# One key load, one copy of the small weights and a new instruction order in a fused sigmoid-attention and token-mixing kernel

## The chip, the cores and the metric

The kernel runs on one core of one Trainium2 chip. The metric is device time in microseconds (us). The profile names the engines PE (TensorE matmul), PEld (TensorE weight load), ACT (ScalarE), DVE (VectorE), POOL (GpSimd) and SP (SyncE, which issues most of the DMAs).

## What is computed

There are 8 batches and 12 heads, 448 tokens and a head size of 64. With `x` the heads side by side (8 x 448 x 768):

```
attn  = sigmoid(q k^T / 8 - log 448)            per batch and head
x     = attn v
W_tok = (x w_q)(x w_k)^T / 8                    w_q, w_k: 768 x 64
out   = relu(W_tok^T x) w_out                   w_out: 768 x 768
```

Inputs and outputs are fp32; the matmuls take bf16.

## The kernel before

The work comes in 24 **pairs**: two batches by two heads, 4 batch pairs with 6 head pairs each. A pair's q, k and v are one 448 KB DMA each (128 partitions, two runs of 1792 bytes per partition). POOL casts each to bf16 (line 118). q and k are then turned on PE (7 transposes of 128x128, line 131) and copied out of PSUM by DVE (line 138).

**Score blocks, S.** A pair has 7. Each is four 64x64 matmuls (one for each half of the rows and columns of the array, line 154) into a PSUM tile of 128x896; ACT makes the sigmoid of it in one instruction (line 159). The text numbers them S0 to S167. **Value blocks, P**, also 7 a pair and also four 64x64 matmuls (line 173), accumulate `attn v`.

After six pairs a batch pair goes through the mixing stage: `x` turned (x, 8 transposes, line 191), the projections W (four 64x64 matmuls each, 12 a batch pair, line 215), N (8 transposes, line 227), U (8 matmuls of 128x64, line 240), M (four 64x64 matmuls, line 264; `m` is the same with the relu on ACT), and O, the product with `w_out` (six 128x128 matmuls of 384 columns, line 283), 14 a batch pair.

**The order on every engine is the order in which the code is written.** A string, `PLAN`, has one letter for each step in PE's order: S, P, q and k (transposes), K (the second part of the first keys' transposes), x, W, N, U, M, O. It has 25 lines, and lines 0 to 23 each hold the 7 S of one pair; line 24 is what remains after the last S. The text speaks of these lines by number.

**PSUM** has three two-bank tiles, shared by S, P, W and M, and two one-bank tiles for the rest.

**Loads.** A second list, `ORDER`, is the order in which SP issues loads and POOL casts them. There are three fp32 buffers for each of q, k and v, so the load of key n waits until key n-3 is cast; there are two bf16 buffers for q and k, so the cast of key n waits until key n-2 has been transposed. SP and POOL take the list strictly in order: a load or cast that must wait holds all that stand behind it. `p_qk` (line 61) holds the transposed q and k.

`w_q` and `w_k` are loaded twice, once into each half of the partitions, with the two halves swapped in columns (lines 326 to 332), and cast at line 406. In the first pair the keys come in two DMAs (lines 352 and 353), of 3 and 4 of the 7 column groups, and are cast in the same two parts by POOL (line 421).

Of the kernel before, what the change touches and what calls it, by code (L numbers as in the profile page):

```python
# [9 lines left out]
F32 = mybir.dt.float32  # L10
# [6 lines left out]
def kernel(  # L17
# [18 lines left out]
    nc = tc.nc  # L36
    B, H, S, HD = q.shape
# [3 lines left out]
    P = 128  # L41
    NI, NP = 7, 64
# [4 lines left out]
    HALF = (slice(0, 64), slice(64, 128))  # L47
# [5 lines left out]
    def pool(name, bufs, **kw):  # L53
        return ctx.enter_context(tc.tile_pool(name=name, bufs=bufs, **kw))

    singles = pool("singles", 1)
# [1 line left out]
    p_w32 = pool("w32", 2)  # L58
    p_c16 = pool("c16", 2)
    p_v16 = pool("v16", 3)  # L60
    p_qk = pool("qk", 8)
    p_at = pool("at", 16)
    p_x = pool("x", 1)
    p_one = pool("one", 1)
# [10 lines left out]
    def bank2(name):  # L75
        n = free2.pop(0)
        return n, ps_q.tile([P, 2, 512], F32, tag=n, name=name)
# [4 lines left out]

    wout16 = singles.tile([P, NC, D], BF16, name="wout16")
    wqk16 = singles.tile([P, H, P], BF16, name="wqk16")
    wqk32 = singles.tile([P, H, P], F32, name="wqk32")
    ident = singles.tile([P, P], F32)
    bias_t = singles.tile([P, 1], F32)
    warm = singles.tile([P, 1], F32)
# [9 lines left out]
    N = len(pairs)  # L98
# [16 lines left out]
    def cast1(n, nm, eng):  # L115
        p = p_v16 if nm == "v" else p_c16
        t16 = p.tile([P, NI, 2, HD], BF16, tag=nm + "16", name=nm + "16")
        eng.tensor_copy(  # L118
            out=t16.rearrange("p i b d -> p b i d"),
            in_=ld.pop((nm, n)).rearrange("p b (i d) -> p b i d", i=NI),  # L120
        )
        ld[nm + "16", n] = t16


    qk = {}
# [24 lines left out]
    def scores(n, i):  # L150
        fb, sc = bank2("sc")
        for b2 in range(2):
            for h in range(2):
                nc.tensor.matmul(  # L154
                    sc[HALF[h], b2, 0:S], qk["k", n][HALF[b2], h, i, :],
                    qk["q", n][HALF[b2], h].rearrange("p i n -> p (i n)"), start=True, stop=True,
                )
        at = p_at.tile([P, 2, S], BF16, tag="at", name="at")
        nc.scalar.activation(at, sc[:, :, 0:S], ACTF.Sigmoid, bias=bias_t, scale=attn_scale)  # L159
        free2.append(fb)  # L160
        ats[n, i] = at
# [46 lines left out]
    def mlp_wqk(u, h):  # L208

        if h == 0:  # L210
            pw[u] = bank2("pw")
        fb, ps = pw[u]
        for b2 in range(2):
            for x in range(2):
                nc.tensor.matmul(  # L215
                    ps[HALF[x], b2, 0:S], wqk16[HALF[b2], h, 64 * x : 64 * x + 64],
                    xts[h // 2][HALF[b2], h % 2, 0:S], start=(h == 0), stop=(h == H - 1),
                )
        if h == H - 1:
            nc.vector.tensor_copy(out=wqk[:, :, 0:S], in_=ps[:, :, 0:S])  # L220
            free2.append(fb)

    def mlp_wkn(u):
        fb, ps = bank([P, 4, 2, P], BF16, "pk")
        for b2 in range(2):
            for m in range(4):
                nc.tensor.transpose(ps[:, m, b2, :], wqk[:, b2, m * P : (m + 1) * P], ident16)  # L227
        wkn[u] = p_one.tile([P, 4, P], BF16, tag="wkn", name="wkn")
        nc.vector.tensor_copy(
            out=wkn[u], in_=ps.rearrange("p m b x -> p m (b x)")[:, :, 64:192]  # L230
        )
        free1.append(fb)
# [91 lines left out]
    w32 = {}  # L324

    def load_weights():
        for b2 in range(2):
            for x, w in enumerate((moe_w_q, moe_w_k)):
                o = 64 * (x ^ b2)
                nc.sync.dma_start(  # L330
                    out=wqk32[HALF[b2], :, o : o + 64], in_=w.rearrange("(h d) n -> d h n", d=HD)
                )

    def load_wout(c):
        w32[c] = p_w32.tile([P, D], F32, tag="w32", name="w32")
        nc.sync.dma_start(out=w32[c], in_=moe_w_out[c * P : (c + 1) * P, :])

    IA, IB = slice(0, 4), slice(4, 7)  # L340
    KA, KB = slice(0, 3), slice(3, 7)
    q0 = p_ld.tile([P, 2, NI * HD], F32, tag="q32", name="q32")
    k0 = p_ld.tile([P, 2, NI * HD], F32, tag="k32", name="k32")
    src = {
        nm: SRC[nm][0:2, 0:2].rearrange("b h (p i) d -> (h p) b (i d)", i=NI) for nm in "qk"
    }

    def cols(r):
        return slice(r.start * HD, r.stop * HD)

    nc.sync.dma_start(out=q0, in_=src["q"])
    nc.sync.dma_start(out=k0[:, :, cols(KA)], in_=src["k"][:, :, cols(KA)])
    nc.sync.dma_start(out=k0[:, :, cols(KB)], in_=src["k"][:, :, cols(KB)])
    nc.vector.memset(zeros, 0.0)
    nc.vector.memset(bias_t, attn_bias)
    nc.gpsimd.memset(ident, 0.0)
# [1 line left out]
        out=ident, in_=ident, compare_op=ALU.not_equal, fill=1.0, base=0,  # L358
# [4 lines left out]
    fb, ps = bank2("pwarm")  # L363
# [4 lines left out]
        nc.vector.memset(t[:, :, S:], 0.0)  # L368


    ORDER = [("q", 1), ("k", 1), ("v", 0)]
    nq = 2
    for n in range(1, N):
        for _ in range(2 if n in (1, 2, 3, 4) else 1):
            if nq < N:
                ORDER += [("q", nq), ("k", nq)]
                nq += 1
        ORDER.append(("v", n))
    for n, at_ in ((0, 18), (1, 30), (2, 33), (3, 36), (4, 39), (5, 42), (6, 45)):
        ORDER.insert(at_, ("w", n))  # L380
    used, loaded, cast = set(), set(), set()

    def pump_loads():
        while len(loaded) < len(ORDER):
            nm, n = ORDER[len(loaded)]
            if nm == "w":
                if n >= 3 and ("w", n - 2) not in cast:
                    break
                load_wout(n - 1) if n else load_weights()
            else:  # L390
                if n >= 3 and (nm, n - 3) not in cast:
                    break
                load1(n, nm, nc.sync)
            loaded.add((nm, n))

    def pump():

        while len(cast) < len(ORDER) + 2:
            nm, n = ORDER[len(cast) - 2]
            if (nm, n) not in loaded:  # L400
                break
            if nm == "w":
                if n:
                    nc.gpsimd.tensor_copy(out=wout16[:, n - 1, :], in_=w32[n - 1])
                else:
                    nc.gpsimd.tensor_copy(out=wqk16, in_=wqk32)
            else:
                back = 3 if nm == "v" else 2
                if n >= back and (nm, n - back) not in used:
                    break  # L410
                cast1(n, nm, nc.gpsimd)
            cast.add((nm, n))
            pump_loads()
# [6 lines left out]
    for t16, t32, r, e in ((q016, q0, IA, "v"), (q016, q0, IB, "s"), (k016, k0, KA, "g"), (k016, k0, KB, "g")):  # L420
        COPY[e](
            out=t16[:, r].rearrange("p i b d -> p b i d"),
            in_=t32[:, :, cols(r)].rearrange("p b (i d) -> p b i d", d=HD),
# [4 lines left out]
    def tr_part(nm, t16, r, e, b=None):  # L428
# [15 lines left out]
    pump()  # L444

    PLAN = (  # L450
        "SSSKqSSSSkq",
        "SPPPPPSkSSPkSPqSS",
        "SxPqSPPPPSPPSqSPPSkPSPP",
        "SxPSSPkSSSkPPSkP",
        "SPPPPSqSqSSqxSxSk",
        "SSqkPPSPPPPSPqSkSSxPPPP",
        "SPPPSkqSWWWSWWWWSWWWWSWSx",
        "SNPSPPPPSPPSUSqSMUmSMq",
        "SkSMxSkSPPPSPPPPSqSk",
        "SMxmqSPPPPSPPPSOSSSOO",  # L460
        "SSkxSSOkSPPPSPPPPSO",
        "SSSqOkSPPPSPPPPSqxSPPPP",
        "SPPPSOSSSqOxSWWWWWSWW",
        "SWWWWWSOSSSNxPPPPPSPPSUU",
        "SMSxkSPPPPSPPPSOSMSkO",
        "SMmOkSMSOqSMSqOSPPPPSPPP",
        "SOSSSkOxSPPPSPPPPSxO",
        "SSSOOSSxOSPPSPPPPPPPPP",
        "SPPPSxqSWSWWWWWWSWWWSWWOS",
        "SSONSSOxSPPPPPPSPSUU",  # L470
        "SSMxOSSPPPPPPPSOSMSkx",
        "SPPPSPPPPmOSMmqOSMSOqSS",
        "SkOxSPPPPSPPPSOSSSOOx",
        "SPSPPPPPPSOSSSOOxS",
        "WPPPWPPPPWWWWWWWWWWOONxOUUMmmOOmMmOOOOOOOOOOOOOOOO",
    )
    done = dict.fromkeys("SPqkKxWNUMO", 0)
    done["q"] = done["k"] = 1

    for t in "".join(PLAN).replace(" ", ""):  # L480
        kind = "M" if t == "m" else t
        c = done[kind]
        done[kind] += 1
        tail = done["S"] == N * NI
        if t == "S":
            scores(*divmod(c, NI))
        elif t == "P":
            n, i = divmod(c, NI)
            values(n, i)
            if i == NI - 1:  # L490
                used.add(("v", n))
                pump()
        elif t in "qk":
            tr(c, t)
            used.add((t, c))
            pump()
        elif t == "K":
            tr_part("k", k016, KB, "v")
        elif t == "x":
            tr_x(c)  # L500
        elif t == "W":
            mlp_wqk(*divmod(c, H))
        elif t == "N":
            mlp_wkn(c)
        elif t == "U":
            mlp_tmp(*divmod(c, 2), tail and c % 2)
        elif kind == "M":
            u, x = divmod(c, NC)
            mlp_mix(u, x, t == "m")
            if x == NC - 1:  # L510
                chunks.extend((u, m, nb) for m in range(NI) for nb in range(2))
        elif t == "O":
            out_chunk(tail)
# [29 lines left out]
```

## Time and profile before

| | |
|---|---|
| median of 7 runs | 210.3 us (209.49 to 212.01) |
| the profiled execution | 210.7 us, span of its instructions 208.9 us |
| PE busy | 197.5 us, 95% of the span |
| ACT busy | 170.6 us, 82%, of it sigmoids 155.2 us (168 of them) |
| DVE, POOL busy | 121.8 us, 72.5 us |
| mean granted TensorE clock | 0.984 |
| q, k, v loads | 24 of each, 448 KB, 7.5 to 8.0 us from issue to landing (median) |

The span begins with the first instruction and ends when the last output has landed. Of the page, the slices (40 of 5.2 us) show how an engine fills over time, the groups give the duration of one instruction, and the chain of waits shows what followed what.

### The profile page before, as it was taken

The page shows a single profiled execution, that of the slowest core. Times are in us where ns is not written, and L with a number is a line of the kernel's source. Part 1 is how long each engine was busy: PE and PEld are TensorE (multiplying, and loading weights), DVE is VectorE, ACT ScalarE, POOL GpSimd, SP SyncE. Part 2 cuts the span into 40 slices and gives each one's busy share as a digit, 9 for nine tenths or more (in the row PEclk, how much of TensorE's full clock was granted, in tenths as well). Part 3 has the DMA queues.
Part 4 walks back from the last instruction along what each step waited for, and adds up shares of the span by engine and source line. Part 5 has one row for each costly group of instructions (what it writes and reads, how often), then busy time and mean ns, then how long its engine had stood idle before and what let it go on. Part 6 is the DMA issues. An engine that isn't in the chain of part 4 may idle for free.

```text
span 208.9 us, 6320 instructions
## 1 busy us (share of the span) xinstructions
PE 197.5 (95%) x2630; PEld 117.9 (56%) x2630; DVE 121.8 (58%) x208; ACT 170.6 (82%) x193; POOL 72.5 (35%) x85
## 2 busy tenths in 40 slices
PE   7489998999999999999999999999999999999991
PEld 7244544666556555656656565656565555655561
DVE  2234645774698755664889674645788654554321
ACT  4687999999999999999998989889888998055220
POOL 2477636877787833730022700251110000000000
PEclk9957999999999999999999999999999999999999
DMA  6999999999999999996064563355213362154785
GB/s 195 374 387 378 380 156 307 384 381 385 383 385 385 380 381 384 397 389 241 5 210 111 158 179 75 78 155 186 58 22 78 75 154 72 23 138 101 201 202 176
DMA packets 28684, 47.59 MB, mean 228 GB/s; under 512 B 5360, under 2 KB 24432, under 8 KB 28656
## 3 DMA queue, kind: packets, MB, share of 16 engines
q1 hardware_dynamic: 27616, 45.03, 67.1%
q10 hardware_dynamic: 1040, 2.16, 2.8%
q8 instruction: 20, 0.33, 0.7%
q14 instruction: 8, 0.07, 0.1%
HBM read 36.18 MB, written 11.01 MB: 226 GB/s over the span
## 4 chain that ended last, share of the span: by engine, by line
PE 83%; ACT 7%; DMA 3%; issue 2%; POOL 2%; SPq 1%; DVE 1%; DVEq 0%; ACTq 0%; POOLq 0%
PE po L283 27%; PE sc L154 18%; PE pv L173 14%; ACT at L159 7%; PE px L191 5%; PE ptq L131 5%; PE ptk L131 4%; PE pw L215 3%; DMA q<-in_q_dram 3%; PE pt L240 3%; PE pm L264 2%; POOL q L118 1%; PE pk L227 1%; DVE o L308 1%; POOL v L118 0%
## 5 line engine op out<-in xcount | busy, mean ns | idle before, releaser
L159 ACT ACTIVATE at<-sc,bias_t 128x896 bf16<-128x896 f32 x168 | 155.2, 1027 | 12.5 <-PE sc L154 11.6
L283 PE MATMUL po<-wout,mx 128*128 128x384 bf16 (+1 forms) x342 | 60.6, 324 | 0.0
L154 PE MATMUL sc<-qt,kt 64*64 64x448 bf16 x672 | 57.6, 364 | 2.8 <-ACT at L159 1.9
L283 PEld LDWEIGHTS <-mx 128*128 128x128 bf16 x342 | 30.9, 98 | 24.3 <-issue 7.0
L173 PE MATMUL pv<-at,v 64*64 64x448 bf16 x672 | 42.7, 358 | 0.3 <-POOL v L118 0.2
L178 DVE CAST xt<-pv 128x896 bf16<-128x896 f32 x24 | 26.2, 1091 | 23.0 <-PE pv L173 23.0
L308 DVE COPY o<-po 128x384 f32<-128x384 f32 x45 | 25.1, 557 | 24.7 <-PE po L283 24.4
L154 PEld LDWEIGHTS <-kt 64*64 64x64 bf16 x672 | 22.3, 105 | 24.2 <-issue 13.3
L118 POOL CAST q<-q 128x896 bf16<-128x896 f32 x23 | 21.5, 933 | 34.2 <-issue 26.3
L118 POOL CAST v<-v 128x896 bf16<-128x896 f32 x24 | 22.3, 934 | 22.5 <-PE pv L173 18.0
L118 POOL CAST k<-k 128x896 bf16<-128x896 f32 x23 | 21.5, 933 | 21.3 <-PE ptk L131 17.7
L173 PEld LDWEIGHTS <-v 64*64 64x64 bf16 x672 | 20.9, 108 | 10.3 <-issue 1.2
L138 DVE COPY kt<-ptk 128x896 bf16<-128x896 bf16 x23 | 14.2, 619 | 10.3 <-PE ptk L131 10.2
L196 DVE COPY xn<-px 128x512 bf16<-128x512 bf16 x48 | 18.0, 416 | 3.1 <-PE px L191 3.0
L306 ACT COPY o<-po 128x384 f32<-128x384 f32 x10 | 4.8, 478 | 15.7 <-PE po L283 15.7
L138 DVE COPY qt<-ptq 128x896 bf16<-128x896 bf16 x23 | 14.1, 618 | 5.7 <-PE ptq L131 5.3
L256 DVE TENSOR_SCALAR mx<-pm 128x896 bf16<-128x896 f32 x15 | 16.3, 1088 | 1.8 <-PE pm L264 1.4
L131 PE MATMUL ptq<-ident,q 128*128 128x128 bf16 x161 | 13.3, 224 | 2.7 <-POOL q L118 2.7
L191 PE MATMUL px<-ident,xt 128*128 128x128 bf16 x192 | 14.7, 220 | 0.2 <-DVE o L308 0.2
L191 PEld LDWEIGHTS <-xt 128*128 128x128 bf16 x192 | 11.6, 98 | 4.7 <-issue 3.9
L131 PEld LDWEIGHTS <-q 128*128 128x128 bf16 x161 | 9.6, 99 | 8.0 <-issue 3.7
L131 PE MATMUL ptk<-ident,k 128*128 128x128 bf16 x161 | 13.7, 228 | 0.0
(43 smaller groups left out, 93.7 us busy)
## 6 DMA issues: line engine op xcount, KB each, us to landing
q<-in_q_dram SPq DMA_DIRECT2D x24, 448.0 KB, 7.7
v<-in_v_dram SPq DMA_DIRECT2D x24, 448.0 KB, 7.5
k<-in_k_dram SPq DMA_DIRECT2D x23, 448.0 KB, 8.0
out_dram<-o SPq DMA_DIRECT2D x44, 192.0 KB, 3.0
w<-in_moe_w_out_dram SPq DMA_DIRECT2D x6, 384.0 KB, 5.8
out_dram<-o ACTq DMA_DIRECT2D x10, 192.0 KB, 3.2
wqk<-in_moe_w_q_dram SPq DMA_DIRECT2D x2, 192.0 KB, 9.5
wqk<-in_moe_w_k_dram SPq DMA_DIRECT2D x2, 192.0 KB, 8.2
```

Of the source, the lines that this page charges most:

```text
L118: eng.tensor_copy(out=t16.rearrange("p i b d -> p b i d"), in_=ld.pop((nm, n)).rearrange("p b (i d) -> p b i d", i=NI),)
L131: nc.tensor.transpose(ps[:, i].rearrange("p h n -> p (h n)"), t16[:, i].rearrange("p b d -> p (b d)"), ident16,)
L138: nc.vector.tensor_copy(out=t[:, hs], in_=ps[:, :, hs, :].rearrange("p i h n -> p h i n"))
L154: nc.tensor.matmul(sc[HALF[h], b2, 0:S], qk["k", n][HALF[b2], h, i, :], qk["q", n][HALF[b2], h].rearrange("p i n -> p (i n)"), start=True, ...
L159: nc.scalar.activation(at, sc[:, :, 0:S], ACTF.Sigmoid, bias=bias_t, scale=attn_scale)
L173: nc.tensor.matmul(ps[HALF[b2], h, 0:S], ld["v16", n][HALF[h], i, b2, :], ats[n, i][HALF[h], b2, :], start=(i == 0), stop=(i == NI - 1),)
L178: nc.vector.tensor_copy(out=xts[j][:, :, 0:S], in_=ps[:, :, 0:S])
L191: nc.tensor.transpose(ps[:, m, h].rearrange("p b d -> p (b d)"), xts[j][:, h, m * P : (m + 1) * P], ident16,)
L196: nc.vector.tensor_copy(out=xns[u][:, :, b2, 2 * HD * j : 2 * HD * (j + 1)].rearrange("p m (h d) -> p m h d", h=2), in_=ps[:, :, :, b2, :],)
L256: nc.vector.tensor_scalar(dst, ps, moe_scale, 0.0, ALU.mult, ALU.max)
L283: nc.tensor.matmul(ps, mxs[u][c].rearrange("p b s -> p (b s)")[:, m * P : (m + 1) * P], wout16[:, c, w0:w1], start=(c == 0), stop=(c == NC ...
L308: nc.vector.tensor_copy(out=o[:, nb * NB : (nb + 1) * NB], in_=ps)
```

## The change

The first keys are one DMA; the two casts of them stay. `w_q` and `w_k` are loaded into the lower 64 partitions only, cast there by POOL (64 partitions instead of 128), and a DMA issued by POOL copies the bf16 result to the upper 64. That copy has the columns unswapped, so in the projection the two column halves change places for the second batch. `p_qk` grows from 8 to 14 buffers. `ORDER` is derived from `PLAN`: each load stands where its tile is first used, and the weights stand some places ahead of their first use. `PLAN` is a new string.

```diff
-    p_qk = pool("qk", 8)
+    p_qk = pool("qk", 14)
...
-    wqk32 = singles.tile([P, H, P], F32, name="wqk32")
+    wqk32 = singles.tile([NP, H, P], F32, name="wqk32")
...
                 nc.tensor.matmul(
-                    ps[HALF[x], b2, 0:S], wqk16[HALF[b2], h, 64 * x : 64 * x + 64],
+                    ps[HALF[x ^ b2], b2, 0:S], wqk16[HALF[b2], h, 64 * x : 64 * x + 64],
...
     def load_weights():
-        for b2 in range(2):
-            for x, w in enumerate((moe_w_q, moe_w_k)):
-                o = 64 * (x ^ b2)
-                nc.sync.dma_start(
-                    out=wqk32[HALF[b2], :, o : o + 64], in_=w.rearrange("(h d) n -> d h n", d=HD)
-                )
+        for x, w in enumerate((moe_w_q, moe_w_k)):
+            nc.sync.dma_start(
+                out=wqk32[:, :, 64 * x : 64 * x + 64], in_=w.rearrange("(h d) n -> d h n", d=HD)
+            )
+
+    def cast_weights():
+        nc.gpsimd.tensor_copy(out=wqk16[HALF[0]], in_=wqk32)
+        nc.gpsimd.dma_start(out=wqk16[HALF[1]], in_=wqk16[HALF[0]])
...
-    nc.sync.dma_start(out=k0[:, :, cols(KA)], in_=src["k"][:, :, cols(KA)])
-    nc.sync.dma_start(out=k0[:, :, cols(KB)], in_=src["k"][:, :, cols(KB)])
+    nc.sync.dma_start(out=k0, in_=src["k"])
...
-    ORDER = [("q", 1), ("k", 1), ("v", 0)]
-    nq = 2
-    for n in range(1, N):
-        for _ in range(2 if n in (1, 2, 3, 4) else 1):
-            if nq < N:
-                ORDER += [("q", nq), ("k", nq)]
-                nq += 1
-        ORDER.append(("v", n))
-    for n, at_ in ((0, 18), (1, 30), (2, 33), (3, 36), (4, 39), (5, 42), (6, 45)):
-        ORDER.insert(at_, ("w", n))
+    STEPS = "".join(PLAN)
+    ORDER, seen = [], dict(q=1, k=1, P=0)
+    first = {}
+    for t in STEPS:
+        if t in "qkP":
+            if t != "P":
+                ORDER.append((t, seen[t]))
+            elif seen[t] % NI == 0:
+                ORDER.append(("v", seen[t] // NI))
+            seen[t] += 1
+        first.setdefault(t, len(ORDER))
+    places = [(first["W"] - 6, 0)] + [(first["O"] - 14 + 2 * c, c) for c in range(1, 7)]
+    for n, (place, c) in enumerate(places):
+        ORDER.insert(place + n, ("w", c))
...
-                    nc.gpsimd.tensor_copy(out=wqk16, in_=wqk32)
+                    cast_weights()
...
     PLAN = (
-        "SSSKqSSSSkq",
-        "SPPPPPSkSSPkSPqSS",
-        "SxPqSPPPPSPPSqSPPSkPSPP",
-        "SxPSSPkSSSkPPSkP",
-        "SPPPPSqSqSSqxSxSk",
-        "SSqkPPSPPPPSPqSkSSxPPPP",
-        "SPPPSkqSWWWSWWWWSWWWWSWSx",
-        "SNPSPPPPSPPSUSqSMUmSMq",
-        "SkSMxSkSPPPSPPPPSqSk",
-        "SMxmqSPPPPSPPPSOSSSOO",
...
-        "WPPPWPPPPWWWWWWWWWWOONxOUUMmmOOmMmOOOOOOOOOOOOOOOO",
+        "SSSKPSkSqSPkSPP",
+        "SPSkSPSPqSqSSxq",
+        "SPPkSqSPPPPSkSPqSPSPP",
+        "SPPPSPkSkSSSqSx",
+        "SqxPSPqSPkSPPPSPqSqSPPP",
+        "SPPPPSqSxSkSSkxPPSPPP",
+        "SkPSPkSqSWWWSkWSWWWSWWWW",
+        "SWkSxSPPPSPNSPPPSUSk",
+        "SMqSqSPPPSPPPPSUSMSx",
+        "SkSMxSqmPPPPSPPPSkSMSqkmPPPP",
...
+        "PPPPWWPPPWWWWWWWWWWOONxOUOUMmMOOMmmOOOOOOOOOOOOOOOO",
     )
```

Counted over the whole plan, the steps are the same (168 S, 168 P, 46 q and k, 24 x, 48 W, 4 N, 8 U, 24 M, 56 O). Neighbours of different tile shape (four 64x64 matmuls on one side, 128x128 or 128x64 on the other) are 156 before and 170 after. The order of the loads becomes q0, k0, v0, k1, q1, k2, k3, q2, q3, q4, v1, k4 and so on; `w_q` and `w_k` stand behind q12 and ahead of k9, where before they stood behind q7, k7 and v3.

More of the change, by code (lines that the diff above doesn't have):

```diff
@@ L336, in load_wout @@
         nc.sync.dma_start(out=w32[c], in_=moe_w_out[c * P : (c + 1) * P, :])
+    PLAN = (
+        "SSSKPSkSqSPkSPP",
[8 more added lines that the diff above has]
+        "SkSMxSqmPPPPSPPPSkSMSqkmPPPP",
+        "SPPPSOSSSkOOSS",
+        "SkOqSPPPPSPPPSOSSSkOx",
+        "SPPPPPSPPSxxSWWSWWWWWWSWWSWWx",
+        "SqSPPPSPPPPSOSSSNOq",
+        "SSUUSPPPPSPPPSOSMSkO",
+        "SMmxxSPPPPSPPPSOSMSOqSM",
+        "SxOSMSOqSSPPPPPPPSOS",
+        "SSqOxSPPPPPSPPSOSPPPSkx",
+        "SPPPWWPWWWSWWWWWWSWSxOSSSNOO",
+        "SSSUUPPSPPPPSPOSMSO",
+        "SMOSMSOSPPPSPPPPSOmMSxx",
+        "SPPPSPPPPSOSMSOxSS",
+        "SOOSPPPPSPPPSOSSSOO",
+        "SPPPPSPPPSOSSSxOxS",
+        "PPPPWWPPPWWWWWWWWWWOONxOUOUMmMOOMmmOOOOOOOOOOOOOOOO",
+    )
     IA, IB = slice(0, 4), slice(4, 7)
@@ L444 @@
     pump()
-    PLAN = (
-        "SSSKqSSSSkq",
-        "SPPPPPSkSSPkSPqSS",
-        "SxPqSPPPPSPPSqSPPSkPSPP",
-        "SxPSSPkSSSkPPSkP",
-        "SPPPPSqSqSSqxSxSk",
-        "SSqkPPSPPPPSPqSkSSxPPPP",
-        "SPPPSkqSWWWSWWWWSWWWWSWSx",
-        "SNPSPPPPSPPSUSqSMUmSMq",
-        "SkSMxSkSPPPSPPPPSqSk",
-        "SMxmqSPPPPSPPPSOSSSOO",
[L461 to L474, printed above, removed]
-        "WPPPWPPPPWWWWWWWWWWOONxOUUMmmOOmMmOOOOOOOOOOOOOOOO",
-    )
     done = dict.fromkeys("SPqkKxWNUMO", 0)
     done["q"] = done["k"] = 1
-    for t in "".join(PLAN).replace(" ", ""):
+    for t in STEPS:
         kind = "M" if t == "m" else t
```

## The prediction

> **What bounds the kernel now.** First the busy times and the slices of the page.
>
> ```profile
> PE 197.5 (95%) x2630; PEld 117.9 (56%) x2630; DVE 121.8 (58%) x208; ACT 170.6 (82%) x193; POOL 72.5 (35%) x85
> PE   7489998999999999999999999999999999999991
> PEclk9957999999999999999999999999999999999999
> ```
>
> PE is full from the fifth slice on. Its empty time lies in the first 20 us and in the last slice. One stretch early on has the half clock (the 5 and the 7): it runs from 11.0 to 17.9 us.
>
> Next, ACT in the window 18.2 to 53.6 us, and four pieces of the chain of waits in order of time (start, length, what).
>
> ```profile
> L159 ACT ACTIVATE at<-sc,bias_t 128x896 bf16<-128x896 f32 x40 | 36.1, 1067 | 0.3 <-PE sc L154 0.2
> 26.28 0.67 ACT at L159
> 27.17 0.78 ACT at L159
> 28.06 0.68 ACT at L159
> ```
>
> From 18.26 us (S9) to 53.7 us (S49, the start of line 7) the sigmoids run without a gap, one each 0.889 us, and PE waits for them. After that PE has more work per line than ACT (lines 7 to 23 last 6.2 to 8.5 us, seven sigmoids 6.2), and only PE counts. So the time is made of three things: when the unbroken row of sigmoids begins, where PE takes over, and how much PE work is left there.
>
> PE's prices are in the same chain:
>
> ```profile
> 72.92 2.06 PE po L283 x12
> 76.92 1.08 PE po L283 x6
> 82.25 0.50 PE ptq L131 x7
> 82.75 0.97 PE po L283 x6
> 83.73 0.39 PE ptk L131 x7
> 85.23 0.76 PE pv L173 x16
> ```
>
> Four 64x64 matmuls cost 0.76/4 = 0.19 us. An O costs 0.97 where a 128x128 step follows and 1.08 where a 64x64 step does; q or k 0.39 and 0.50. So each change of tile shape costs 0.11. In the same way x costs 0.45, N 0.45, U 0.65. Check: before has 408 blocks of four (77.1), 46 q and k (18.0), 24 x and 4 N (12.5), 56 O (54.6), 8 U (5.2), in all 167.5, and 156 changes (17.2), 184.6 in all; first score block at 6.1, last output landed 4.1 after PE ends. That leaves 14.1 of the 208.9 as lost PE time, 10 of it in lines 0 to 3.
>
> The loads, by POOL's casts:
>
> ```profile
> 8.68 0.93 POOL L118 CAST q<-q 128x896 bf16<-128x896 f32 x1 [2.02 <-DMA q<-in_q_dram]
> 9.86 0.93 POOL L118 CAST k<-k 128x896 bf16<-128x896 f32 x1 [0.25 <-DMA k<-in_k_dram]
> 11.07 0.93 POOL L118 CAST v<-v 128x896 bf16<-128x896 f32 x1 [0.28 <-DMA v<-in_v_dram]
> 12.18 0.93 PE L131 MATMUL ptk<-ident,k 128*128 128x128 bf16 x7
> 33.67 1.47 POOL L406 CAST wqk<-wqk 128x1536 bf16<-128x1536 f32 x1 [0.56 <-DMA wqk<-in_moe_w_k_dram]
> ```
>
> One load lands each 1.20 us, whichever it is. The PE row shows seven transposes at half clock, 0.93 from first start to last end.
>
> **Part by part. First keys.** Before, the two casts began at 4.74 and 6.04, and S0 1.35 after the first, at 6.09. One load lands no earlier than 4.16 + 1.20 = 5.36 (4.16 is the cast of q0) and no later than 6.04; I take 5.7, so S0 comes at 7.05, 1.0 later. That is covered: S3 waited for a load until 10.60, and S0 to S2 now end at 10.2. The next load can be cast at 8.5 (bigger packets, 0.2).
>
> **The first two lines.** The third load is now v0, cast by 9.45; P stands ahead of S3 and waits for it, S3 starts on ACT at 10.3 (before 10.60). Then k1, q1, k2, k3 are cast by 10.65, 11.85, 13.05, 14.25. From k1 to S9 PE has 4 transposes, 9 blocks of four and 7 changes: 1.57 + 1.71 + 0.77 = 4.05 us at full clock. It begins at 10.7; 0.3 passes at full clock, and the rest, 3.7, needs 7.4 at half clock, of which the window to 17.9 holds 3.4. S9 is issued at 18.1 to 18.2 and starts on ACT at 18.3. Before, it was 18.26. The values done early fill the hole, but do not move the row. I take 18.3; were the window short, S9 could come at 16.5, S3 and six sigmoids (10.3 + 5.3 = 15.6) with a load late.
>
> **Where PE takes over.** S(n) is due at 18.3 + 0.889(n - 9). Before, from line 7 on: 305 blocks (57.6), 24 q and k, 18 x, 4 N, 8 U, 56 O, 108 changes, 148.6 in all; 53.7 + 148.6 = 202.3. After, the lines ahead hold less than 6.2 each until line 9, which begins with S63, due at 66.3; from there 275 blocks, 16 q and k, 17 x, 3 N, 6 U, 56 O, 94 changes, 136.0; 66.3 + 136.0 = 202.3 as well. The 14 changes more (14 x 0.11 = 1.5) are in this; they are paid for by 3 us less of PE idling in lines 0 to 6. Before, PE lost another 0.6 in lines 7 and 8, after its takeover; after, these two lines still lie under ACT's row, where such a loss costs nothing. So: -0.6.
>
> **The weights.** Two DMAs fewer:
>
> ```profile
> 21.45 0.75 SPq L330 DMA_DIRECT2D wqk<-in_moe_w_q_dram  x1
> 26.98 3.56 SPq L330 DMA_DIRECT2D wqk<-in_moe_w_k_dram  x1
> 188.83 0.50 ACTq L318 DMA_DIRECT2D out_dram<-o  x1
> ```
>
> They held SP and the queue from 21.45 to 30.5, inside the unbroken row, so halving them gains nothing. The cast keeps its 1.47 (1536 elements per partition either way). New on POOL is the issue of the copy. No row shows a DMA issued by POOL. Lower end 0.47 to 0.50, an issue of SP, or of ACT with 64 packets of 3 KB like this one; upper end 3.56, the longest issue of these weights. I take 1.2, the geometric mean of 0.47 and 3.56 (1.3) drawn towards the ACT row.
>
> Behind it on POOL stand the casts of k9, k10, v5, k11, k12 and q13. SP can issue q12 when q9 is cast, after q7 is transposed (line 3, about 32.5): 33.9. `w_k` follows at 34.9. From issue to landing a load took 3.3 to 5.3 in 100 to 160 us, where the queue is not full; I take 5.3: 40.2. Cast to 41.7, issue to 42.9, k9 cast by 43.85. PE wants k9 behind S38, at 43.6. That is 0.25 late. But k12 shares k9's buffer: its load waits for this cast, 43.9, lands after 4.3 (the median of those loads) and 0.5 of the copy ahead of it at 48.7, is cast by 49.65, transposed by 50.15, and S44, behind it on PE, starts at 50.5 instead of 49.4; q13, cast behind k12, adds 0.2. Together 1.3 late at S45, in a stretch where ACT has no slack. With an issue of 0.47 it is 0.6, with 3.56 it is 3.7. The copy itself is needed by the first W, behind S45, and lands by 46.9 (3.5 for a single key load): covered by 3 us; without that cover W would wait on PE.
>
> The Trainium skill ("SBUF - State Buffer", section "A bandwidth-pool intuition that's wrong") speaks against this copy: a GpSimd-issued DMA of 620 ns took about 3100 ns beside a VectorE copy that holds their shared port. Here all 24 casts of v on POOL took 933 to 935 ns, with DVE busy two thirds of the time, so no such hold is seen; by the rule, as an estimate, the issue would be 2.5 us longer and the time 213.5. The skill's "DMA: Bandwidth & Descriptors" ("Anatomy of one DMA") gives such a DMA 2.0 us and its bytes over 436 GB/s, as an estimate 2.45 us for 196,608 bytes; by that the copy lands 1 us earlier, and the sum is the same.
>
> **The rest has one answer.** `p_qk` with 14 buffers costs nothing. The other order of column halves in W leaves four matmuls on four quarters of the array, 0.19. The tail keeps its kinds; one O more in line 24 is one fewer before.
>
> **The sum.** -0.6 + 1.3 = +0.7: span 209.6, this execution 211.4 instead of 210.7. The median is 0.4 under the profiled execution, so 211.0. The measurement of this kernel can tell about 0.5% (1.05 us) from no change; +0.7 is inside.
>
> **Rivals.** A: the ramp does gain. If the half-clock window is shorter or PE does better in it, S9 comes up to two sigmoids earlier (1.8): 209.2. For it: casts of k1 to k3 are ready by 14.25, and only PE's clock holds S9. Against it: PE stands still from 7.2 to 9.45 as it did before (7.2 to 9.66), the same ahead of the half clock; and 28 loads at 1.20 plus the weights (2.8) end at 43.7, where an earlier row would meet its loads.
>
> B: slower. POOL's issue of the copy is long, and k9, then k12, are late by it one for one. From 1.55 us on it is slower by over 0.5%; at 3.56 the time is 213.4. For it: nothing in these lines has slack and POOL takes its list in order. Against it: the nearest row, 0.50.
>
> C: the change does not act: row and takeover as before, no stall on POOL: -0.6 or 0, 209.7 to 210.3.
>
> **How the numbers follow.** Forecast with C 0.45 (within 0.5%), A 0.15, B 0.40, since k9 to q13 have several more ways of being late than early. The range reaches from A, with 0.2 below it for the spread of the runs, 209.0, nearly to B's end, 213.2; the likeliest case alone is 209.7 to 211.4.
>
> **What would show it.** S9 at 18.3; 0.25 us of PE waiting for POOL's k cast near 43.6 and about 1 near 49; POOL's issue 1.2; changes 0.11 each; line 9 near 67.5 and then PE full. Wrong if S9 comes before 17.4, if the k casts wait for their loads and not for the copy, or if PE waits after line 9.

## The result and the profile after

The changed kernel takes 213.99 us (median of 12 runs, 211.99 to 216.14), the kernel before 210.3 us on the same chip (31 runs). The ratio is 1.0152, 95% interval [1.0122, 1.0182]: it is slower by 1.5%, where the prediction had +0.3% (211.0) and a range of 209.0 to 213.2. The ratio, here and in the experiments, is taken over the runs in the faster of two states that executions fall into, and is not the quotient of the two medians (213.99 / 210.3 = 1.018). The profiled execution took 212.87 us with a span of 211.0, against 210.7 and 208.9. It is 1.1 us quicker than its kernel's median, and that of before was 0.4 slower than its own, so the two traces differ by 2.2 us where the medians differ by 3.7.

The page after, busy times, PE's slices and the granted clock:

```profile
PE 199.5 (95%) x2630; PEld 116.8 (55%) x2630; DVE 124.2 (59%) x210; ACT 169.2 (80%) x191; POOL 73.1 (35%) x86
PE   7699999969999999999999999999999999999991
PEclk9769999979999999999999999999999999999997
```

Two things differ from before. The ramp is better: PE is at 9 from the third slice on, where before it was from the fourth, and the early half-clock stretch lies at 7.42 to 14.25 us instead of 11.0 to 17.9. But the ninth slice (42.2 to 47.5 us) has a 6 in PE and a 7 in the clock, where before has 9 in both. ACT's sigmoids there, from the timeline (start, duration, line, operation, count; in brackets the idle time ahead and what ended it):

```profile
41.96 2.80 ACT L159 ACTIVATE at<-sc,bias_t 128x896 bf16<-128x896 f32 x3 [0.17 <-ACT at L159]
46.64 1.90 ACT L159 ACTIVATE at<-sc,bias_t 128x896 bf16<-128x896 f32 x2 [1.88 <-PE sc L154]
49.37 1.01 ACT L159 ACTIVATE at<-sc,bias_t 128x896 bf16<-128x896 f32 x1 [0.82 <-PE sc L154]
```

The row of sigmoids begins with S6 at 14.75, which puts S9 at 17.43, 0.8 earlier than in before; but it breaks after 44.8, where before's ran to 53.7. PE's timeline at the break:

```profile
42.81 0.38 PE L154 MATMUL sc<-qt,kt 64*64 64x448 bf16 x4
45.08 0.93 PE L131 MATMUL ptk<-ident,k 128*128 128x128 bf16 x7 [1.89 <-POOL k L118]
```

and the chain of waits through the same moment:

```profile
33.45 0.74 SPq L328
34.24 7.31 DMA wqk<-in_moe_w_k_dram
41.67 1.47 POOL wqk L333
43.14 0.29 issue
43.44 0.65 POOL wqk L334
44.08 0.95 POOL k L118
45.08 0.93 PE ptk L131 x7
```

This is the place that the prediction named: `w_k` lands (41.55), POOL casts the weights, issues the copy, casts k9, and PE, which wanted k9 at 43.19, gets it at 45.08. From the start of the weights' cast to PE's transposes are **3.41 us**, and PE wanted k9 1.52 after that start. The seven transposes then take 0.93, the half-clock figure. The windows view (busy us and instructions of PE, PEld, DVE, ACT, POOL; granted clock; DMA share; GB/s) has line 5 in its first row and the half-clock stretch in its second:

```profile
40.00:49.65 9.65, 7.76 (x105) 4.84 (x104) 4.49 (x9) 6.78 (x8) 6.91 (x8) 0.82 0.92 289
44.97:48.38 3.41, 3.30 (x30) 2.37 (x30) 1.21 (x2) 1.74 (x2) 2.67 (x4) 0.50 0.79 224
```

With PE's prices line 5 is 5.98 us of work and lasts 9.61. In the kernel without weights, below, the same line lasts 6.57, so the pause of 1.9 us and the 3.4 us at half clock behind it cost 3.0 us together. Lines 6 to 22 lose 1.5 us together, with the weights and without.

The weights are not all that came late: k9's own load stands behind them on the queue and landed at 42.56. Cast at once it would have reached PE at about 43.6 (0.93 for the cast, 0.1 for the steps around it), still 0.4 after PE wanted it; the other 1.5 are POOL's.

### The profile page after: what moved, and what is told of

It is laid out like the page before. It is cut to its first block, busy times and chain, and to the rows that moved or that the text cites. A ratio compares the mean times of both kernels' runs of the same rounds, so it can differ in the third digit from the quotient of the medians.

```text
span 211.0 us, 6277 instructions
## 1 busy us (share of the span) xinstructions
PE 199.5 (95%) x2630; PEld 116.8 (55%) x2630; DVE 124.2 (59%) x210; ACT 169.2 (80%) x191; POOL 73.1 (35%) x86
## 2 busy tenths in 40 slices
DMA packets 26891, 47.38 MB, mean 225 GB/s; under 512 B 3792, under 2 KB 22608, under 8 KB 26864
## 4 chain that ended last, share of the span: by engine, by line
PE 81%; DMA 7%; ACT 4%; POOL 2%; SPq 1%; issue 1%; DVE 1%; DVEq 0%; ACTq 0%; POOLq 0%
PE po L283 27%; PE sc L154 17%; PE pv L173 13%; PE px L191 5%; PE ptk L131 5%; PE pw L215 4%; PE ptq L131 4%; ACT at L159 4%; DMA wqk<-in_moe_w_k_dram 3%; DMA k<-in_k_dram 3%; PE pt L240 3%; PE pm L264 3%; POOL k L118 1%; PE pk L227 1%; POOL wqk L333 1%
## 5 line engine op out<-in xcount | busy, mean ns | idle before, releaser
L154 PE MATMUL sc<-qt,kt 64*64 64x448 bf16 x672 | 59.4, 369 | 1.6 <-ACT at L159 1.0
L173 PE MATMUL pv<-at,v 64*64 64x448 bf16 x672 | 43.3, 353 | 0.6 <-ACT at L159 0.4
L173 PEld LDWEIGHTS <-v 64*64 64x64 bf16 x672 | 20.3, 107 | 10.2 <-issue 1.2
L256 DVE TENSOR_SCALAR mx<-pm 128x896 bf16<-128x896 f32 x17 | 18.4, 1088 | 1.9 <-PE pm L264 1.8
L131 PE MATMUL ptk<-ident,k 128*128 128x128 bf16 x161 | 14.4, 236 | 2.2 <-POOL k L118 2.2
L131 PEld LDWEIGHTS <-k 128*128 128x128 bf16 x161 | 10.2, 105 | 9.4 <-POOL k L118 4.5
```

What stands on the lines that cost most here:

```text
L131: nc.tensor.transpose(ps[:, i].rearrange("p h n -> p (h n)"), t16[:, i].rearrange("p b d -> p (b d)"), ident16,)
L154: nc.tensor.matmul(sc[HALF[h], b2, 0:S], qk["k", n][HALF[b2], h, i, :], qk["q", n][HALF[b2], h].rearrange("p i n -> p (i n)"), start=True, ...
L173: nc.tensor.matmul(ps[HALF[b2], h, 0:S], ld["v16", n][HALF[h], i, b2, :], ats[n, i][HALF[h], b2, :], start=(i == 0), stop=(i == NI - 1),)
L256: nc.vector.tensor_scalar(dst, ps, moe_scale, 0.0, ALU.mult, ALU.max)
```

## The experiments

The theory that came out of this trace: a list "by first use" has no lead, so the 3.41 us chain of weights, cast, copy issue and k cast stops PE, and the clock drops behind the pause. The rival: the new instruction order, with 14 more changes of tile shape, costs the time by itself. Unless said otherwise each edit is to the kernel after.

**The weights earlier in the list.** They stand at item 25 (counted from 0); here at 19.

```diff
-    places = [(first["W"] - 6, 0)] + ...
+    places = [(first["W"] - 12, 0)] + ...
```

> The weights' load, cast and copy stand twelve places ahead of their first use instead of six; nothing else differs from the changed kernel. Theory 1 (the weights land late and hold POOL's list, so k9 comes late, PE pauses about 2 us near 43 us, and the half clock that follows costs as much again): the pause and the half clock near 45 us are gone, line 5 loses 0.5 instead of 3.6 us, 210.5 to 211.5 us. Theory 2 (the new order with its 14 more changes of tile shape and its longer look-ahead costs the time, the pause is only where it shows): 213 us or more, the loss comes up elsewhere.

Measured: 215.33 us, ratio 1.0215 [1.0152, 1.0277]. GpSimd's and PE's timelines, the rows on the path:

```profile
37.27 1.46 POOL L333 CAST wqk<-wqk 64x1536 bf16<-64x1536 f32 x1 [1.55 <-DMA wqk<-in_moe_w_k_dram]
39.03 0.65 POOL L334 DMA_DIRECT2D wqk<-wqk  x1 [0.30 <-POOL wqk L333]
40.68 0.93 PE L131 MATMUL ptq<-ident,q 128*128 128x128 bf16 x7 [4.14 <-POOL q L118]
```

The theory had 210.5 to 211.5 us here and missed; the time and the place of the loss are as the rival had them, and the run without weights below decides between the two. The pause did not go, it moved: now q9 stands behind the weights and PE waits 4.14 us for it in line 4, with 6.8 us of half clock from 37.18. Line 5 loses only 0.5. The chain is again 3.41 us (37.27 to 40.68). An earlier place alone makes an earlier pause, since each item of the list is needed about as soon as it comes.

**The weights loaded twice, no copy**, as in before, at the place that they have after.

```diff
-        nc.gpsimd.tensor_copy(out=wqk16[HALF[0]], in_=wqk32)
-        nc.gpsimd.dma_start(out=wqk16[HALF[1]], in_=wqk16[HALF[0]])
+        for b2 in range(2):
+            for x, w in enumerate((moe_w_q, moe_w_k)):
+                o = 64 * (x ^ b2)
...
-                    cast_weights()
+                    nc.gpsimd.tensor_copy(out=wqk16, in_=wqk32)
```

> The changed kernel with the weights loaded twice and cast at full width, without the copy, as in the kernel before, at the changed kernel's place in the lists. Theory 1: two more DMAs of 1.4 us each land the weights 2 to 3 us later, the copy's 0.65 plus 0.3 us on POOL is saved, so k9 is 1 to 2 us later than in the changed kernel: 215 to 216 us. Rival (it is the POOL-issued copy itself that costs): faster than the changed kernel by 1 us or more, 213 or less.

Measured: 214.35 us, 1.0201 [1.0142, 1.0261]. The time lies between the theory's range and the rival's. In PE's timeline the same wait, longer, and POOL's casts ahead of it:

```profile
47.30 0.93 PE L131 MATMUL ptk<-ident,k 128*128 128x128 bf16 x7 [3.40 <-POOL k L118]
43.10 1.47 POOL L440 CAST wqk<-wqk 128x1536 bf16<-128x1536 f32 x1 [1.67 <-DMA wqk<-in_moe_w_k_dram]
46.31 0.93 POOL L118 CAST k<-k 128x896 bf16<-128x896 f32 x1 [1.74 <-DMA k<-in_k_dram]
```

The last of four loads landed at 42.95, 1.4 later than the last of two. But POOL was done with the weights at 44.57 and then stood still for 1.74 us: here k9's cast waits for its own load. SP was held by the four issues (the last took 2.90 us) and issued k9 at 40.08 instead of 35.59; it landed at 46.26. So it is the queue of loads, not POOL, that ends this wait, and the issue that POOL saves gains nothing. Loading once is no loss against loading twice.

**The kernel before with the weights loaded once** and copied, at before's place (item 18 of before's list).

```diff
-    wqk32 = singles.tile([P, H, P], F32, name="wqk32")
+    wqk32 = singles.tile([NP, H, P], F32, name="wqk32")
...
-                    nc.gpsimd.tensor_copy(out=wqk16, in_=wqk32)
+                    cast_weights()
```

> The kernel before with only the weights changed: loaded once, cast on 64 partitions, copied by a POOL-issued DMA, at its own early place (behind q7, k7, v3). Theory 1: POOL has room there, weights land 3 us sooner than before, 210.0 to 210.6 us, no change. Rival (a POOL-issued DMA costs wherever it stands): 211.3 us or more.

Measured: 210.92 us, 1.001 [0.9975, 1.0045]: no change. Its rows on POOL and PE are the most telling of all:

```profile
34.00 1.46 POOL L333 CAST wqk<-wqk 64x1536 bf16<-64x1536 f32 x1 [1.71 <-DMA wqk<-in_moe_w_k_dram]
35.77 0.65 POOL L334 DMA_DIRECT2D wqk<-wqk  x1 [0.30 <-POOL wqk L333]
37.41 0.56 PE L131 MATMUL ptq<-ident,q 128*128 128x128 bf16 x7 [0.37 <-POOL q L118]
```

POOL waits even longer for the weights (1.71 against 1.36), the chain from cast to transposes is the same 3.41 us (34.00 to 37.41), and PE waits 0.37. What differs at this place is the lead: here PE wants the tile 3.04 us after the cast began, in the kernel after 1.52. (Plan and list differ too, so this comparison by itself doesn't single the lead out.)

**First keys in two loads again.**

```diff
-    nc.sync.dma_start(out=k0, in_=src["k"])
+    nc.sync.dma_start(out=k0[:, :, cols(KA)], in_=src["k"][:, :, cols(KA)])
+    nc.sync.dma_start(out=k0[:, :, cols(KB)], in_=src["k"][:, :, cols(KB)])
```

> The changed kernel with the first keys in two loads again. Theory 1: S0 comes 1 us sooner, but S3 waits for the next load anyway, and everything behind is 0.2 us later: 213.8 to 214.5 us. Rival (the later S0 is part of the loss): 213 us or less.

Measured: 214.05 us, 1.0183 [1.012, 1.0245], not to be told from the kernel after; PE's wait for k9 was 2.44 us in this execution. The first keys have no part in the loss.

**No weights at all**: no loads, no cast, no copy; the bf16 weights are a constant. This is the test between theory and rival.

```diff
+    nc.gpsimd.memset(wqk16, 0.01)
...
-                load_wout(n - 1) if n else load_weights()
+                if n:
+                    load_wout(n - 1)
...
-                else:
-                    cast_weights()
```

> The kernel after, with the two weight loads, their cast and the copy to the other half left out; the weights on chip are filled with a constant at the start, so the gating scores are not the reference's. Everything else (order, first keys, 170 changes of tile shape) stays. Theory (the loads and casts have no lead, GpSimd stands still for the late weights at 40.3 to 41.7 us, k9 is cast late and TensorE pauses 1.9 us before it and then runs at half clock for 3.4 us): the pause before k9 goes, line 5 of the plan loses under 1 us in place of 3.6, no half-clock stretch after 20 us, time 209.5 to 210.8 us. Rival (the new order with its more frequent changes of tile shape costs the time by itself): 212.5 to 214 us still.

Measured: 210.0 us, 0.9986 [0.9952, 1.0021]. The page's clock has only the early stretch, and PE's transposes of k9 wait for nothing:

```profile
PEclk9859999999999999999999999999999999999998
```

```profile
43.24 0.56 PE L131 MATMUL ptk<-ident,k 128*128 128x128 bf16 x7
```

Line 5 loses 0.58 and line 9 begins at 65.59 us instead of 68.44. The rival falls: without the weights the new order, with all its changes of tile shape, is as fast as the old one.

**The control**, before without weights.

```diff
+    nc.gpsimd.memset(wqk16, 0.01)
...
-                load_wout(n - 1) if n else load_weights()
+                if n:
+                    load_wout(n - 1)
...
-                else:
-                    nc.gpsimd.tensor_copy(out=wqk16, in_=wqk32)
```

> The control: the kernel before with its weight loads and cast left out in the same way (gating scores not the reference's). Theory: in the kernel before the weights stood on no path (TensorE waited for nothing there), so 209.8 to 210.8 us, no change from the kernel before. Rival (weights cost something in any kernel, through the transfers): 208.5 to 209.5 us.

Measured: 210.04 us, 1.0001 [0.9963, 1.0039]. In before the weights cost nothing, so loading and casting them is no loss by itself; it takes the place in the list.

**Before with the list by first use**: before's plan, everything loaded as in before, the weights six places ahead of the first W, which is item 22.

```diff
-    ORDER = [("q", 1), ("k", 1), ("v", 0)]
...
+    places = [(first["W"] - 6, 0)] + [(first["O"] - 14 + 2 * c, c) for c in range(1, 7)]
```

> The kernel before with its own plan, first keys in two loads and weights loaded twice, but with the list of loads taken from the change: ordered by first use in the plan, weights six places ahead of their first use. Theory (it is the list by first use that takes the lead away from the casts): TensorE now pauses somewhere between 15 and 45 us for a cast, with half clock behind it, and the time is 212.5 to 216 us. Rival (the list alone is harmless; the new plan is what costs): 209.8 to 211 us.

Measured: 215.17 us, 1.0267 [1.0202, 1.0331]. On POOL and PE:

```profile
40.48 1.47 POOL L437 CAST wqk<-wqk 128x1536 bf16<-128x1536 f32 x1 [1.75 <-DMA wqk<-in_moe_w_k_dram]
42.00 0.93 POOL L118 CAST v<-v 128x896 bf16<-128x896 f32 x1
42.99 0.96 PE L173 MATMUL pv<-at,v 64*64 64x448 bf16 x8 [3.63 <-POOL v L118]
```

The old plan with the new list makes the same kind of loss, with v4 in the place of k9 and no copy in the chain. Half clock from 41.14 to 47.97. v4's own load, behind the weights on the queue, landed at 41.95, just as POOL was done with them, so here queue and cast are late by the same. So it is the list by first use with the weights in it that does it, in either plan.

**Loads early, cast late.** The weights' loads stand nine places ahead of the first W, their cast seven.

```diff
-    places = [(first["W"] - 6, 0)] + ...
+    places = [(first["W"] - 9, 7), (first["W"] - 7, 0)] + ...
...
+                if n == 7:
+                    load_weights()
```

> The kernel after with the weights loaded nine places ahead of their first use in the list and cast seven places ahead of it, in place of both at six: the loads start earlier, and GpSimd reaches the cast later after them. Theory (GpSimd's wait for the late weights is what delays the casts): GpSimd's wait ahead of the weights' cast falls from 1.36 us to under 0.5, the pause before k9 falls under 0.5 us, no half clock at 45 us, time 210 to 211.5 us. Rival (the list has no lead at all, whichever transfer is late stops TensorE; the pause moves to another cast as it did with twelve places): 213 to 215.5 us.

Measured: 212.45 us, 1.0116 [1.0061, 1.0171]. POOL no longer waits ahead of the weights' cast, and no half clock follows, but PE still stops twice:

```profile
39.29 0.56 PE L131 MATMUL ptq<-ident,q 128*128 128x128 bf16 x7 [1.04 <-POOL q L118]
43.70 0.56 PE L131 MATMUL ptq<-ident,q 128*128 128x128 bf16 x7 [1.40 <-POOL q L118]
```

The theory's numbers missed, and so did the rival's (213 us and more): the one pause of 1.89 became two of 1.04 and 1.40, without half clock. The interval overlaps that of the kernel after, so a gain is not certain. The first wait is for a q whose load stood behind the weights on the queue (landed 38.15, cast from 38.30), the second for a q whose cast stood behind them on POOL (cast from 42.70). What the weights gained within the list, another tile lost.

**Bigger packets.** The weights read in runs of 3 KB in place of 256 bytes.

```diff
-    wqk32 = singles.tile([NP, H, P], F32, name="wqk32")
+    wqk32 = singles.tile([NP, 2, H, NP], F32, name="wqk32")
...
-                out=wqk32[:, :, 64 * x : 64 * x + 64], in_=w.rearrange("(h d) n -> d h n", d=HD)
+                out=wqk32[:, x], in_=w.rearrange("(d h) n -> d h n", d=HD)
...
```

> The kernel after, with the two weights read as runs of 3 KB per partition in place of twelve runs of 256 bytes (the rows then stand in another order, so the gating scores are not the reference's). Bytes, place in the list, cast and copy stay. Theory A (it is the time that the small packets hold the transfer engines that makes the hole in the loads): the last weight lands by 40.5 us, the pause before k9 falls under 0.7 us, no half clock behind it, time 210 to 211.5 us. Rival (GpSimd's 2.4 us for cast and issue are enough by themselves, since the list has no lead): the pause stays at 1.5 to 2.5 us and the time at 213 to 214.5 us.

Measured: 213.15 us, 1.0115 [1.0073, 1.0158]. Packets under 512 bytes fell from 3792 to 2256, but `w_k` landed at 41.24, against 41.55, not by 40.5. Of the issues view, the kernel after and then this one, and PE's pause before k9:

```profile
wqk<-in_moe_w_k_dram SPq DMA_DIRECT2D x1, 192.0 KB, 7.3
wqk<-in_moe_w_k_dram SPq DMA_DIRECT2D x1, 192.0 KB, 6.5
44.77 0.56 PE L131 MATMUL ptk<-ident,k 128*128 128x128 bf16 x7 [0.88 <-POOL k L118]
```

The cast began at 41.36 and the chain took 3.41 again. This execution ran 0.7 us later up to line 5, loads included (v4, the last but one ahead of the weights, landed at 37.37 instead of 36.62), and PE wanted k9 later (43.89). Counted from v4's landing `w_k` came after 3.87 us instead of 4.93: the small packets cost about 1 us of the landing here, one execution each. Another 1.6 us was lost in line 8, which the kernel after does not lose, in a wait for a v; why it was late was not looked into. So the packets are a part of what makes the weights late, not all of it, and the shorter pause had no half clock behind it. Both theories had a part of it wrong.

**Before's plan, list by first use, weights at item 18.**

```diff
-    places = [(first["W"] - 6, 0)] + ...
+    places = [(first["W"] - 10, 0)] + ...
```

(against the kernel with the weights at item 22)

> As e8_before_jit, the kernel before with its own plan and the list of loads by first use, but with the weights (still loaded twice) put at item 18, where the list of before has them; e8 had them at item 22. Theory A (with before's plan, which asks for 22 items by the end of line 4 against 26 in the plan of after, the list by first use is bad only where the weights stand late in it): 209.8 to 211.2 us, no pause over 1 us after line 3. Rival (the order of the other loads by first use takes the lead by itself): 212.5 to 215 us.

Measured: 211.67 us, 1.006 [1.0028, 1.0092], between the two. Four items earlier bring back about three quarters of the loss (2.07 of 2.67 points of the ratio); the wait of 3.63 became two of 0.58 and 0.60. The list by first use keeps about 0.6% of its own. In this plan an earlier place helps, in the plan of after it did not: by the end of line 4 that plan has used 26 tiles of q, k and v by 40.0 us, the old one 22 by 40.5.

**What might be worth keeping**: before with the first keys in one load and the weights loaded once.

```diff
-    nc.sync.dma_start(out=k0[:, :, cols(KA)], in_=src["k"][:, :, cols(KA)])
-    nc.sync.dma_start(out=k0[:, :, cols(KB)], in_=src["k"][:, :, cols(KB)])
+    nc.sync.dma_start(out=k0, in_=src["k"])
```

(with the weights as in the kernel "before with the weights loaded once")

> A version meant to keep what is good of the change: the kernel before, its plan and its list, with the first keys in one load and the weights loaded once and copied on chip. Theory A: no pause is added after line 3 and the first lines are as in before, so 209.6 to 210.6 us, within half a per cent of before, at best 0.3 per cent faster. Rival (one load for the first keys makes the first S wait longer in this plan, whose first line takes the first half of the keys alone): 211 to 212 us.

Measured: 211.24 us, 1.0024 [0.9998, 1.005]. Nothing is gained, and the time is in the rival's range, but not for its reason: S0 came at 7.31 instead of 6.09, and by line 2 that was made up (20.80 instead of 21.31). Line 5 then lost 0.7 us against before, 0.61 of it in a wait for a q. PE ended only 0.16 us later than in before; the other 1.2 us of the longer span lie behind its last instruction (5.40 us instead of 4.21, and 5.29 in before without weights), which neither theory touches. No version that loads the weights beats the kernel before.

**Cast and copy without the loads.** What is POOL's part, what the loads'?

```diff
+    nc.gpsimd.memset(wqk32, 0.01)
...
-                load_wout(n - 1) if n else load_weights()
+                if n:
+                    load_wout(n - 1)
```

> The kernel after with the two weight loads alone left out; the tile that they fill is set to a constant at the start, so the gating scores are not the reference's. The cast (1.46 us), the copy's issue (0.30 + 0.65 us) and the copy itself stay at their place in GpSimd's list. Theory (the hole in the loads is the larger part of the pause, GpSimd's 2.4 us the smaller): GpSimd no longer waits ahead of the cast, the pause before k9 falls to at most 0.7 us, no half clock behind it, time 210 to 211 us. Rival (GpSimd's 2.4 us are the pause, whatever the loads do, as big_packets hinted): a pause of 1 to 2 us remains and the time is 212 to 213.5 us.

Measured: 210.98 us, 1.0038 [1.0003, 1.0072].

```profile
38.05 0.94 POOL L118 CAST q<-q 128x896 bf16<-128x896 f32 x1 [0.56 <-PE ptq L131]
38.93 1.46 POOL L333 CAST wqk<-wqk 64x1536 bf16<-64x1536 f32 x1
40.69 0.65 POOL L334 DMA_DIRECT2D wqk<-wqk  x1 [0.30 <-POOL wqk L333]
41.34 1.82 POOL L118 CAST k<-k 128x896 bf16<-128x896 f32 x2
```

```profile
42.58 0.56 PE L131 MATMUL ptk<-ident,k 128*128 128x128 bf16 x7
```

Cast, issue and copy are all there, but the cast begins straight behind q11's, at 38.93 instead of 41.67; 38.93 + 3.41 = 42.34 is before PE's 42.58, and PE does not wait. With the two loads the ratio is 1.0152, without them 1.0038, without cast and copy too 0.9986: some two thirds of the loss (1.14 of 1.66 points) come from the loads, the rest from POOL's time. "The loads" takes in the loads behind them on the queue: k9's landed at 38.86 here. The three intervals are each 0.3 to 0.35 points to either side, so the shares are rough, and the profiled execution was the quickest of its kernel (209.53, at full clock throughout).

## Why the prediction was wrong

**The place was right, the size was not.** The prediction had the weights' chain delaying k9 on PE in line 5, and no wait after line 9. That is what happened. It said 0.25 us of waiting at k9; it was 1.89. As for the sign, its +0.7 us was called too small to tell from no change.

**The step that failed is "The weights", in its term for the loads.** `w_k` was to be issued at 34.9 and land 5.3 later, at 40.2. Its issue began at 34.24, a little earlier, and it took 7.31: 41.55. The 5.3 was taken from 100 to 160 us, "where the queue is not full". At 34 us it is full: in the issues view (count, KB, median us from issue to landing) the weights of before took this long, too, and those were the rows to use.

```profile
wqk<-in_moe_w_q_dram SPq DMA_DIRECT2D x2, 192.0 KB, 9.5
wqk<-in_moe_w_k_dram SPq DMA_DIRECT2D x2, 192.0 KB, 8.2
```

With 8.2 the same working gives 43.1 for the landing and a wait of about 3 us. (That is more than the 1.89 measured.) One part of the late landing is in the trace: the 16 transfer engines do not finish together. Of `w_k` the middle engine was done at 39.41 and the last at 41.55, and the last is what counts. The 1.64 us by which the wait was longer than forecast are 1.35 of later landing and 0.41 by which PE came to k9 earlier (43.19 for 43.6), less 0.25 that the copy's issue was cheaper; 0.13 are gaps between the steps. The experiment without the loads agrees that the loads, not POOL's time, are the larger part.

**A term that was missing is the clock.** The sum charged a pause with its length. In the profiled execution 1.9 us of pause was followed by 3.4 us at half clock, and line 5 lasted 3.0 us longer than without weights: another 1.1. That is the profiled execution, not the whole loss: in eight of the twelve runs the granted clock was 0.971 or 0.972 as there, in four 0.981 to 0.997, and the run at 0.997, which leaves 2 x 0.003 x 212.7 = 1.3 us of half clock, took 214.57 us. Where that run lost its time no trace shows.

The Trainium skill, "TensorE: Matmul & The Clock Gate", section "What's actually happening", has the half clock return after at least one idle window of about 3.4 us; the stretches here are indeed 3.41 and 6.83 us long, but PE had stood still for only 1.78 us when this one began (43.19 to 44.97), so half clock came after a shorter idle time than that rule has.

**The copy itself was right or better.** The issue was taken at 1.2 and took 0.65 with 0.30 ahead of it, in all eight kernels that have it, so rival B's mechanism (a long issue) is out, although k9 was late and its end, 213.4, was passed. By the skill's warning on GpSimd's DMAs beside VectorE ("SBUF — State Buffer", section "A bandwidth-pool intuition that's wrong") the issue would, as an estimate, have been 2.5 us longer; the 0.65 shows nothing of it in any of these runs. The copy landed 3.2 us after its issue began, where the first key load had suggested 3.5. The estimate from the skill's "DMA: Bandwidth & Descriptors" (section "Anatomy of one DMA") was 2.45. The copy was covered, and so it was with the queue full, where it took 7.3, as below (landed at 42.97, first W at 49.79). k12 landed at 48.47 for 48.7, but by luck: its load was issued 1.15 us later than forecast and took 3.42 instead of 4.8, and PE was late already.

**"First keys" held.** Its cast began at 5.69 for 5.7 and S0 came at 7.04 for 7.05; to the hundredth that is luck, since S0 came at 6.69 to 7.31 in the other kernels with one load for the first keys. The next load was to be cast at 8.5, with 0.2 for bigger packets in it: its cast began at 7.76 here and at 7.66 to 8.91 in the experiments on this kernel with one load, a spread in which no run shows the 0.2.

**"The first two lines" were wrong for the better.** S9 was to start on ACT at 18.3, held by a half-clock window to 17.9; it started at 17.43. The window lay at 7.42 to 14.25 in this execution; in those of the experiments it lay between 8.3 and 15.9, or there was none. It is not a thing to build a step on. Rival A, an earlier row of sigmoids, had this part right. By itself this made line 9 start 0.7 us earlier than the 66.3 of the sum (65.59 without weights). The saving of 0.6 in the next step did not come, so the sum of both is about what the prediction had, by luck.

**"Where PE takes over" held, apart from its -0.6.** Line 9 starts at 68.44 with the weights and 65.59 without. From there to the end of the span are 142.5 us, where the priced work and the last landing give 136.0 + 4.1; in before, from line 7, 155.2 against 148.6 + 4.1. Both are 2.4 to 2.5 above the price: before loses 0.6 of it in lines 7 and 8, the kernel after 0.7 in line 9. The prices themselves (0.19, 0.97, 0.11 a change) fit lines 10 to 22 to 0.4 us of 93.6. The counts of changes, 156 and 170, take in neighbours O and U (one before, three after), at which both sides are wider than 64x64; the trace has about 0.10 for these too.

So the profiled span is 209.6 as predicted, - 0.7 from the ramp, + 1.55 from the weights (2.85 in place of 1.3, line 9 with the weights against without), + 0.55 for the saving that did not come: 211.0, as measured. The median execution lost 1.1 more than the profiled one. That part was not seen in a trace of this kernel and its cause stays open; the kernels with the first keys in two loads and with the weights loaded twice paused 2.4 and 3.4 us before k9 in their profiled executions, and a pause like that would do it.

## What to carry to other kernels

In both plans here a list ordered strictly by first use had no slack at the weights: what matters for each item is the time between its landing and its need, and one late item ahead of it in a strict queue stops all behind it. Before moving a transfer, follow the chain from its landing to the first consumer that stands behind it (here 3.41 us) and compare it with the lead in the trace (3.04 in the kernel before with the weights loaded once, 1.52 in the kernel after); look also at when that consumer's own load lands. Take the transfer's time from rows of the same stage of the kernel, with the queue as full. And where half clock follows a PE pause, charge more than its length: here 3.0 us for 1.9.

## What the runs showed of the hardware

- **Half clock behind a short pause.** Pauses of PE of 1.89, 2.44, 3.40, 3.63 and 4.14 us were followed by half clock (3.41, 3.41, 6.83, 6.83 and 6.83 us); behind waits of 0.6 to 1.4 us after line 3 none was seen, but for the last of these five, where a wait of 1.38 us came just ahead. The stretch can begin while PE still stands. In the first 16 us the length of the last pause does not tell: the stretch at 7.42 us in the kernel after followed waits of 1.15 and 0.45 us, and in before it began 1.4 us after the end of a wait of 2.48, with a further wait of 0.73 just begun.
- **One DMA, two prices.** The GpSimd-issued copy of 192 KB landed 3.1 us after its issue began where the transfers moved 174 GB/s, and 7.3 us where they moved 349 (the windows view over these stretches). Of the issues view, first the kernel without the weight loads, then before with one key load and weights once:

```profile
wqk<-wqk POOLq DMA_DIRECT2D x1, 192.0 KB, 3.1
```

```profile
wqk<-wqk POOLq DMA_DIRECT2D x1, 192.0 KB, 7.3
```

- **The last transfer engine decides.** Of the loads that landed between 28 and 42 us in the kernel after, the last of the 16 engines ended 1.4 to 2.5 us behind the middle one; over all kernels it was 0.3 to 5.0. For `w_k` it was 2.1, and 1.5 with runs of 3 KB (39.76 and 41.24).
